# A fused attention and feed-forward kernel: the row of k's maxima is spread over the partitions by two DMAs through DRAM, not by four transposes, in batches 1 to 7

## The chip, the cores and the metric

The kernel runs on one core of one Trainium2 chip. The metric is the device time of one execution in microseconds (us); lower is better. The time before the change is the median of three runs.

## The reference

The reference is a linear attention (softmax of q over the head dimension, softmax of k over the sequence) followed by a two-layer feed-forward part. Cut to what matters:

```python
# q, k, v: (batch 8, heads 8, seq 576, head_dim 64), float32
q_s = softmax(q, axis=-1)                       # over the 64 of a head
k_s = np.exp(k - np.max(k, axis=2, keepdims=True))   # max over the sequence:
k_s = k_s / (np.sum(k_s, axis=2, keepdims=True) + 1e-9)  # one per batch, head, d
kv  = einsum('bhsd,bhse->bhde', k_s, v)
x   = einsum('bhsd,bhde->bhse', q_s, kv)        # to (4608, 512)
h   = x @ w_in                                  # 512 -> 2048
g   = h * erf(softplus(h))
out = g @ w_out                                 # 2048 -> 512
```

For each batch, the maximum of k over the sequence is 512 numbers: 8 heads of 64.

## The kernel before

**Work.** Tokens lie on the partitions when k and q are loaded: a batch has 576 tokens, 512 of them as 128 partitions x 4 and a tail of 64 that shares a tile with the other batch of its pair. Attention of a batch gives columns of x, already transposed; the feed-forward part takes them in blocks of 384 tokens, 12 blocks in all, each in 4 groups of the hidden dimension. That makes 48 items `n`. An item has a first product (`mm1`, lines 911 and, for the first four, 950), softplus and erf on ScalarE (both L343), a product on VectorE (L991) with two splittings into halves of 16 bits (L1005, L1009), and a second product (`mm2`, lines 1037 and 1028) that comes two items later. `mm1` multiplies blocks by Strassen's scheme of seven products; its PSUM banks are called pX, pY and pZ, with one buffer each. VectorE and ScalarE empty them into the tile H, and the next product of that bank waits for it: ScalarE's copies are L928, L930 and L938, VectorE's are L923, L925, L933 and L936.

**Order.** Batch 0 and the first four items are written out by hand in a list of steps. From there a loop over the items calls a generator, `attention`, which yields after each step of a batch; `pace` takes as many steps after each part of `mm2` as a table of shares sets. The tile framework then orders the instructions of each engine itself by a planner, so that a row can stand in another place than in the code; after that each engine runs its own list strictly in order. DMAs of activations, and the stores of the output, are all issued by SyncE (SP), one list as well.

**The steps of one batch around the change**, in `attention` (L639 on):

- `k_max` takes the maximum over the four tokens of each partition and the tail on VectorE (L496 to L500): a tile `kmax` of 128 x 512.
- `k_max_T` transposes `kmax` on TensorE in four pieces into a PSUM bank `kT` (L507); VectorE reduces that bank over the tokens (L511) to `km`, 128 x 4: column c, partition p holds the maximum of entry 128c + p.
- `k_max_rows` transposes each column of `km`, repeated 128 times, by four further transposes on TensorE into a PSUM bank `kB` (L520): every partition then holds the whole row of 512 maxima.
- VectorE subtracts `kB` from both halves of k, `k_0` and `k_1` (L654), and from the tail `kt` (L659). Between L511 and this stands whatever the planner put there.
- ScalarE takes the exponentials of `k_0`, `k_1`, `kt`, `q_0`, `q_1` and, for an odd batch, of the tail of q, `qt` (all L343).
- TensorE multiplies them with v into the banks `kv_0` and `kv_1` (L541; `kt` enters as `kv<-vtail,kt`).

The small PSUM tiles (`kT`, `kB`, `kv`, `qT`, `x` and so on) share two banks, tag `bk`. The tile `kmax`, its helper `k2` and the later `kvf` and `qTs` share two SBUF buffers, tag `qT`. Batch 0 takes the same functions by its own list of steps.

Of the kernel before, what the change touches and what calls it, by code (L numbers as in the profile page):

```python
# [9 lines left out]
F32 = mybir.dt.float32  # L10
# [46 lines left out]
def attn_moe_kernel(  # L57
# [9 lines left out]
    nc = tc.nc  # L67
    B, H, S, D = q.shape
    NTOK, DM = out.shape
    DFF = w_in.shape[1] // 2  # L70
    P = 128
# [4 lines left out]
    NC4 = DM // P  # L76
# [7 lines left out]
    GE = FG * T  # L84

    cp = ctx.enter_context(tc.tile_pool(name="cp", bufs=1))
    ch = ctx.enter_context(tc.tile_pool(name="ch", bufs=1))
    at = ctx.enter_context(tc.tile_pool(name="at", bufs=2))
    xp = ctx.enter_context(tc.tile_pool(name="xp", bufs=2))
# [248 lines left out]
    def act(out_, in_, func, chain=True, **kw):  # L338

        with ExitStack() as es:  # L340
            if chain and last[0] is not None:
                es.enter_context(tc.issue_after(last[0]))
            i = nc.scalar.activation(out_, in_, func, **kw)  # L343
        if chain:
            last[0] = i.ins
        return i
# [91 lines left out]
    def bank(name):  # L438
        return psa.tile([P, 512], F32, tag="bk", name=name)
# [4 lines left out]
    def hd(t):  # L444
        return t.rearrange("p h d -> p (h d)")

    def rows(t):
        return t.rearrange("p t h d -> p (t h) d")

    def q_sub(t, g, name):  # L450

        m = at.tile([P, g], F32, tag=f"qm{g}", bufs=1, name=f"{name}_m")
        nc.vector.tensor_reduce(m, t, axis=AX.X, op=ALU.max)
        nc.vector.tensor_tensor(
            t, t, m[:, :, None].to_broadcast([P, g, D]), op=ALU.subtract
        )
# [34 lines left out]
    def k_max(b, ks, kt):  # L491

        kmax = at.tile([P, H, D], F32, tag="qT", name=f"kmax_{b}")
        k2 = at.tile([P, 2, 4, D], F32, tag="qT", name=f"k2_{b}")
        for hf in range(2):
            nc.vector.tensor_tensor(k2, ks[hf][:, 0:2], ks[hf][:, 2:4], op=ALU.max)  # L496
            nc.vector.tensor_tensor(
                kmax[:, hf * 4:hf * 4 + 4, :], k2[:, 0], k2[:, 1], op=ALU.max
            )
        nc.vector.tensor_tensor(kmax[kt[1]], kmax[kt[1]], kt[0], op=ALU.max)  # L500
        return kmax

    def k_max_T(b, kmax):
        bk = bank(f"kT_{b}")
        km2 = hd(kmax)
        for c in range(NC4):
            nc.tensor.transpose(  # L507
                bk[:, c * P:(c + 1) * P], km2[:, c * P:(c + 1) * P], ident
            )
        km = at.tile([P, NC4], F32, tag="km", bufs=1, name=f"km_{b}")  # L510
        nc.vector.tensor_reduce(  # L511
            km, bk.rearrange("p (c s) -> p c s", c=NC4), axis=AX.X, op=ALU.max
        )
        return km

    def k_max_rows(b, km):

        bk = bank(f"kB_{b}")
        for c in range(NC4):
            nc.tensor.transpose(  # L520
                bk[:, c * P:(c + 1) * P], km[:, c:c + 1].to_broadcast([P, P]), ident
            )
        return bk.rearrange("p (h d) -> p h d", h=H)

    W = D + 1

    def kv_mm(b, hf):


        d, kt_ = bat[b], bat[b - b % 2]["kt"]  # L530
        bk = bank(f"kv_{b}_{hf}")
        for c in range(2):
            for t in range(TM + 1):
                for a in range(2):
                    h = 2 * c + a
                    if t < TM:
                        kk, vv = d["k"][hf][:, t, h, :], d["v"][hf][:, h, t, :]
                    else:

                        kk, vv = kt_[:, 4 * hf + h, :], vtail[:, 4 * hf + h, :]  # L540
                    nc.tensor.matmul(  # L541
                        bk[a * D:(a + 1) * D, c * W:(c + 1) * W], kk, vv,
                        start=(t == 0), stop=(t == TM),
                    )
        return bk
# [7 lines left out]
    def kv_norm(b, hf, bk):  # L553
        if b >= E32:
            if hf == 0:
                bat[b]["kvf"] = at.tile([P, NC4, D], F32, tag="qT", name=f"kvf_{b}")
            kvf = bat[b]["kvf"]
        bkv = bk[:, :2 * W].rearrange("p (c w) -> p c w", c=2)
        rd = at.tile([P, 2, 1], F32, tag="rd", bufs=1, name=f"rd_{b}_{hf}")
        nc.vector.tensor_scalar_add(rd, bkv[:, :, D:], 1e-9)  # L560
        nc.vector.reciprocal(rd, rd)
        cs = slice(2 * hf, 2 * hf + 2)
        if b >= E32:
            nc.vector.tensor_tensor(
                kvf[:, cs, :], bkv[:, :, :D], rd.to_broadcast([P, 2, D]), op=ALU.mult
            )
            return
        for a in range(2):
            ps = slice(a * D, (a + 1) * D)
            nc.vector.tensor_tensor(  # L570
                kv32[b][ps, cs, ps], bkv[ps, :, :D], rd[ps].to_broadcast([D, 2, D]),
                op=ALU.mult,
            )
# [68 lines left out]
    def attention(b):  # L642
        d, j, p = bat[b], b % 2, b // 2
        even = bat[b - j]
        tl = slice(j * TAIL, (j + 1) * TAIL)
        ks, qs, kt = d["k"], d["q"], even["kt"][tl]
        kmax = k_max(b, ks, (kt, tl))
        yield SHARES[0]
        km = k_max_T(b, kmax)
        q_sub(rows(qs[0]), 16, f"q_{b}_0")  # L650
        yield SHARES[1]
        kb = k_max_rows(b, km)
        for hf in range(2):
            nc.vector.tensor_tensor(  # L654
                ks[hf], ks[hf],
                kb[:, None, hf * 4:hf * 4 + 4, :].to_broadcast([P, TM, 4, D]),
                op=ALU.subtract,
            )
        nc.vector.tensor_tensor(kt, kt, kb[tl], op=ALU.subtract)  # L659
        yield SHARES[2]  # L660
        q_sub(rows(qs[1]), 16, f"q_{b}_1")
        if j == 1:
            q_sub(even["qt"], H, f"qt_{p}")
        yield SHARES[3]
        for t in (*ks, kt, qs[0], qs[1], *([even["qt"]] if j == 1 else [])):
            act(t, t, AF.Exp, chain=b > 1)
        yield SHARES[4]
        kv_norm(b, 0, kv_mm(b, 0))
        d["v"].append(load_half(v, "v", b, 1))
        q_norm(rows(qs[0]), 16, f"q_{b}_0", b)  # L670
        yield SHARES[5]
        kv_norm(b, 1, kv_mm(b, 1))
        if b + 1 < B:
            load_kv(b + 1)
        mx = kv_max(b)
        yield SHARES[6]
        kv_split(b, mx)
        yield SHARES[7]
        q_norm(rows(qs[1]), 16, f"q_{b}_1", b)
        if j == 1:  # L680
            q_norm(even["qt"], H, f"qt_{p}", b)
        yield SHARES[8]
        for i in ((3 * p + 1, 3 * p + 2) if j else (3 * p, 3 * p + 1)):
            while not x_free(i):
                yield 0
        if j == 1:
            qt2 = hd(even["qt"])
            bk = bank(f"qTt_{p}")
            for c in range(NC4):
                nc.tensor.transpose(  # L690
                    bk[:, c * P:(c + 1) * P], qt2[:, c * P:(c + 1) * P], ident
                )
            qT = q_evac(b, bk, f"qTt_{p}")
            if b + 1 < B:
                even_next = bat[b + 1]
                even_next["qt"] = load_tail(q, "qt", p + 1)
            yield SHARES[9]
            bk = bank(f"xt_{p}")
            x = xblock(p * NBK + 1)
            bk3 = bk.rearrange("p (c s) -> p c s", c=NC4)  # L700
            for a in range(2):
                for c in range(NC4):
                    cs = slice(c * P + a * TAIL, c * P + (a + 1) * TAIL)
                    x_mm(2 * p + a, c, bk[:, cs], qT[:, :, cs])
            for a in range(2 if b < E32 else 1):
                w = TAIL if b < E32 else P
                o = SM - T + a * TAIL
                x_put(
                    bk3[:, :, a * TAIL:a * TAIL + w], x[:, :, o:o + w],
                    bat[a]["sx"] if b < E32 else None,  # L710
                )
            yield SHARES[10]
        for c in range(NC4):
            hf, c2 = divmod(c, 2)
            qT = q_T(b, c, bank(f"qT_{b}_{c}"))
            if c2 == 1 and b + 1 < B:
                load_q(b + 1, hf)
            yield SHARES[11]
            bk = bank(f"x_{b}_{c}")
            x_mm(b, c, bk, qT)  # L720
            x_split(b, c, bk)
            if c == NC4 - 1:
                d["xdone"] = True
            yield SHARES[12]
# [464 lines left out]
```

## Time and profile before

| | |
|---|---|
| time, median of three runs | 862.84 us |
| the three runs | 860.36, 862.84, 862.9 us |
| span of the profiled execution, first to last instruction | 860.3 us |
| TensorE busy, share of the span | 825.6 us, 96% |
| VectorE busy | 637.1 us, 74% |
| ScalarE busy | 504.2 us, 59% |
| GpSimd busy | 17.6 us, 2% |
| mean DMA traffic | 65 GB/s |
| granted TensorE clock, mean over the span | 0.989 |

No time is recorded for the profiled execution by itself. Its span, from the first to the last instruction, is 0.1 us under the fastest of the three runs and 2.6 us under their median. In the rows of a timeline the first column is the start in us from the span's start and the second the time that the row lasts, with consecutive equal instructions merged; what stands in brackets at the end is the idle time of that engine ahead of the row and what ended it. Ends of matmuls are modelled and overlap the next instruction, so how long TensorE was really held by a group is read from the start of the group to the start of what follows. A group of matmuls in float32 counts two instructions for one in the code; the transposes count one.

### The profile page before, as it was taken

The numbers are of one execution on the slowest core, as the hardware profiler recorded it, in microseconds if no ns is written. First come the engines' busy times: TensorE is split into PE (matmuls) and PEld (weight loads), VectorE is DVE, ScalarE is ACT, GpSimd is POOL, SyncE is SP. The second block draws the span as 40 slices with busy tenths as digits, with TensorE's granted clock in tenths as the row PEclk, the third lists the DMA queues.
The fourth block names the chain that finished last, engine by engine and source line by source line (L and its number), as shares of the span: only waits on it lengthen the run. The fifth ranks groups of instructions, "written<-read, shape, count | busy, mean of one in ns | idle before, by whom it ended". The sixth has DMA issues, their size and how long they took to land.

```text
span 860.3 us, 15503 instructions
## 1 busy us (share of the span) xinstructions
PE 825.6 (96%) x6532; PEld 569.2 (66%) x6532; DVE 637.1 (74%) x921; ACT 504.2 (59%) x645; POOL 17.6 (2%) x37
## 2 busy tenths in 40 slices
PE   3999997999999999999999999999999999999997
PEld 2655556676766776776776677767776677777673
DVE  6899889998886779759866779858866656653543
ACT  2597677866554566565664466466655466453532
POOL 2010000000000000000000000000000000000000
PEclk8999999999999999999999999999999999999999
DMA  9996320032123302311140202311110000100100
GB/s 273 397 268 178 100 75 13 19 88 50 37 54 77 87 1 50 93 28 24 50 105 14 68 19 51 80 38 26 32 32 2 25 13 2 37 2 1 37 2 37
DMA packets 117381, 55.53 MB, mean 65 GB/s; under 512 B 106560, under 2 KB 108608, under 8 KB 117312
## 3 DMA queue, kind: packets, MB, share of 16 engines
q1 hardware_dynamic: 115136, 46.15, 20.6%
q0 software_dynamic: 2176, 8.39, 2.7%
q8 instruction: 51, 0.84, 0.4%
q14 instruction: 18, 0.15, 0.1%
HBM read 45.09 MB, written 9.44 MB: 63 GB/s over the span
## 4 chain that ended last, share of the span: by engine, by line
PE 67%; DVE 17%; ACT 10%; issue 2%; DMA 2%; SPq 1%; POOL 0%; ACTq 0%; DVEq 0%; POOLq 0%
PE o L1037 31%; PE pX L911 16%; PE pZ L911 8%; ACT G L343 4%; PE pY L911 4%; ACT L343 3%; PE kv L541 2%; DVE G L991 2%; PE x L631 2%; PE qT L616 2%; DVE H L1009 1%; DVE x L297 1%; PE o L1028 1%; DVE wi L297 1%; DVE H L1005 1%
## 5 line engine op out<-in xcount | busy, mean ns | idle before, releaser
L1037 PE MATMUL o<-wo,H 128*128 128x512 f16 x1512 | 348.0, 379 | 1.7 <-DVE H L1005 1.3
L911 PEld LDWEIGHTS <-wi 128*128 128x128 f16 x3696 | 309.5, 98 | 39.0 <-issue 17.4
L1037 PEld LDWEIGHTS <-H 128*128 128x128 f16 x1512 | 145.7, 98 | 150.1 <-DVE H L1005 1.8
L911 PE MATMUL pX<-x,wi 128*128 128x192 f16 x2112 | 204.8, 247 | 6.4 <-ACT H L930 3.0
L343 ACT ACT_TABLE_LOAD x104 | 133.4, 1283 | 8.5 <-DVE H L936 5.3
L991 DVE SCALAR_TENSOR_TENSOR G<-G,small,H 128x1536 f32<-128x1536 f32 x44 | 80.0, 1818 | 65.8 <-ACT G L343 65.5
L911 PE MATMUL pZ<-x,wi 128*128 128x192 f16 x1056 | 102.9, 246 | 0.9 <-DVE H L936 0.5
L938 ACT COPY H<-pX 128x384 f32<-128x384 f32 x44 | 20.9, 476 | 138.0 <-PE pX L911 133.0
L343 ACT ACTIVATE G<-H,U 128x768 f32<-128x768 f32 (+1 forms) x60 | 72.9, 1231 | 24.4 <-DVE H L936 23.8
L1009 DVE TENSOR_TENSOR H<-G,H 128x1536 f16<-128x1536 f32 x42 | 73.8, 1757 | 1.1
L343 ACT ACTIVATE G<-G 128x1536 f32<-128x1536 f32 x48 | 71.2, 1484 | 0.5
L1028 PE MATMUL o<-wo,G 128*128 128x512 f32 x144 | 66.7, 604 | 0.0
L911 PE MATMUL pY<-x,wi 128*128 128x192 f16 x528 | 51.8, 248 | 1.6 <-DVE H L923 1.6
L442 ACT ACTIVATE x<-x 128x384 f32<-128x384 f32 (+1 forms) x52 | 17.6, 386 | 54.4 <-PE x L631 51.9
L923 DVE COPY H<-pY 128x384 f32<-128x384 f32 x44 | 24.4, 554 | 31.4 <-PE pY L911 31.3
L1028 PEld LDWEIGHTS o<-wo,G 128*128 128x128 f32 x144 | 26.3, 193 | 26.5 <-issue 25.8
L297 DVE SCALAR_TENSOR_TENSOR x<-x,x 128x768 f16<-128x768 f32 (+1 forms) x44 | 37.1, 850 | 5.8 <-ACT x L296 5.7
L1005 DVE CAST H<-G 128x1536 f16<-128x1536 f32 x42 | 40.1, 955 | 0.7
L296 ACT ACTIVATE x<-x 128x768 f16<-128x768 f32 (+1 forms) x44 | 32.9, 761 | 11.4 <-DVE x L387 11.4
L1053 DVE TENSOR_SCALAR ob<-o,V 128x512 f32<-128x512 f32 x29 | 21.7, 748 | 23.1 <-PE o L1037 23.1
L936 DVE TENSOR_TENSOR H<-pZ,H 128x384 f32<-128x384 f32 x44 | 24.3, 552 | 19.3 <-PE pZ L911 19.3
L925 DVE TENSOR_TENSOR H<-pX,H 128x384 f32<-128x384 f32 x44 | 24.4, 555 | 15.3 <-PE pX L911 14.9
(182 smaller groups left out, 804.2 us busy)
## 6 DMA issues: line engine op xcount, KB each, us to landing
out_dram<-ob SPq DMA_DIRECT2D x32, 256.0 KB, 2.3
vbuf<-in_v_dram SPq DMA_DIRECT2D x60, 128.0 KB, 3.1
q<-in_q_dram SPq DMA_DIRECT2D x56, 128.0 KB, 3.2
k<-in_k_dram SPq DMA_DIRECT2D x56, 128.0 KB, 3.3
wo<-in_moe_w_in_dram SPq DMA_DIRECT2D x4, 1024.0 KB, 16.9
wi<-in_moe_w_out_dram POOLq DMA_DIRECT2D x2, 1024.0 KB, 8.3
wi<-in_moe_w_in_dram SPq DMA_DIRECT2D x2, 1024.0 KB, 8.0
raw<-in_moe_w_out_dram POOLq DMA_DIRECT2D x2, 1024.0 KB, 7.9
```

What stands on the lines that cost most here:

```text
L296: nc.scalar.activation(hi, src, AF.Copy, scale=s)
L297: nc.vector.scalar_tensor_tensor(lo, src, s, hi, op0=ALU.mult, op1=ALU.subtract)
L343: i = nc.scalar.activation(out_, in_, func, **kw)
L911: nc.tensor.matmul(o, w[wl][:, c, a * P:(a + 1) * P], x[:, xl, xi, c, :], start=(new and a == 0 and c == 0 and i == 0), stop=(c == 1 and i ...
L923: nc.vector.tensor_copy(C[0, 0], bank2("Y"))
L925: add(C[0, 0], bank2("X"), C[0, 0], op=ALU.add)
L936: add(C[0, 1], bank2("Z"), C[0, 1], op=ALU.add)
L991: nc.vector.scalar_tensor_tensor(flat(s["G"]), flat(s["G"]), (GB if n in OUT32 else GA)[:, g:g + 1], flat(s["H"]), op0=ALU.mult, op1=ALU.mult,
L1005: nc.vector.tensor_copy(flat(s["gh"]), flat(s["G"]))
L1009: nc.vector.tensor_tensor(flat(s["gl"]), flat(s["G"]), flat(s["gh"]), op=ALU.subtract)
L1028: nc.tensor.matmul(o, s["G"][:, a, ts_], w[:, a, :], start=(first_ and a == 0), stop=(last_ and a == FG - 1),)
L1037: nc.tensor.matmul(o, s[gt][:, a, ts_], w[wl][:, a, :], start=(first_ and a == 0 and i == 0), stop=(last_ and a == FG - 1 and i == 2),)
```

## The change

A DRAM pool with two buffers is added. For batches 1 to 7, `k_max_rows` and its four transposes are replaced by `k_max_spread`, which is called right after `k_max_T`: SyncE stores `km` to a row of 512 numbers in DRAM, and then loads this row into all 128 partitions of a new SBUF tile `kB`. Batch 0 keeps the four transposes.

```diff
+    dr = ctx.enter_context(tc.tile_pool(name="dr", bufs=2, space=bass.MemoryType.DRAM))
...
+    def k_max_spread(b, km):
+
+        row = dr.tile([1, DM], F32, tag="km", name=f"kmd_{b}")
+        nc.sync.dma_start(row.rearrange("o (c p) -> (o p) c", c=NC4), km)
+        kb = at.tile([P, DM], F32, tag="qT", name=f"kB_{b}")
+        nc.sync.dma_start(kb, row.to_broadcast([P, DM]))
+        return kb.rearrange("p (h d) -> p h d", h=H)
...
         kmax = k_max(b, ks, (kt, tl))
         yield SHARES[0]
         km = k_max_T(b, kmax)
+        kb = k_max_spread(b, km)
         q_sub(rows(qs[0]), 16, f"q_{b}_0")
         yield SHARES[1]
-        kb = k_max_rows(b, km)
         for hf in range(2):
```

The subtraction therefore reads `kB` from SBUF and not from PSUM, and waits for a DMA and not for TensorE. `kB` takes one more turn in the two buffers `qT`, and the turn of `kB` in the two PSUM banks `bk` is gone. On SP the two DMAs stand ahead of the loads of v's second half, and in batches 5 and 7 ahead of four stores of the output. Lines after the new function have moved by nine or ten.

The planner also moves other rows. In batches 2, 3, 4 and 6 the order on VectorE between the reduction L511 and the subtractions is the same as before. At three places other rows change.

ScalarE in batch 5, from the erf of an item (`G<-G`) to the exponentials of that batch and the copies of the banks pZ and pX into H. Before:

```order
L343 ACTIVATE G_3916<-G_3916 128x1536
L928 COPY H_3920<-pZ_3985 128x2x192
L343 ACT_TABLE_LOAD
L343 ACTIVATE k_0_3185<-k_0_3185 128x1024
L930 COPY H_3920<-pX_3935 128x2x192
L343 ACTIVATE k_1_3190<-k_1_3190 128x1024
L343 ACTIVATE kt_2213<-kt_2213 64x512
L343 ACTIVATE q_0_3478<-q_0_3478 128x1024
L343 ACTIVATE q_1_3659<-q_1_3659 128x1024
L343 ACTIVATE qt_2358<-qt_2358 128x512
L938 COPY H_3920<-pX_3935 128x2x192
```

And now (L344 is the L343 of before, L937, L939 and L947 are L928, L930 and L938):

```order
L344 ACTIVATE G_3918<-G_3918 128x1536
L344 ACT_TABLE_LOAD
L344 ACTIVATE k_0_3183<-k_0_3183 128x1024
L344 ACTIVATE k_1_3188<-k_1_3188 128x1024
L344 ACTIVATE kt_2212<-kt_2212 64x512
L344 ACTIVATE q_0_3476<-q_0_3476 128x1024
L344 ACTIVATE q_1_3657<-q_1_3657 128x1024
L344 ACTIVATE qt_2357<-qt_2357 128x512
L937 COPY H_3922<-pZ_3982 128x2x192
L939 COPY H_3922<-pX_3937 128x2x192
L947 COPY H_3922<-pX_3937 128x2x192
```

The copies of pZ and of the first pX have moved from among the exponentials to behind all six of them; batch 7 has the same move.

TensorE at the same place, from the last `mm2` product of an item (bank `o_2`) to `kv_0`. Before, the pX product that waits for the copy L930 stood between `o_1` and `o_2`, further up:

```order
L1037 MATMUL o_2_3551<-wo_95,H_3603 128x512
L541 MATMUL kv_0_4062<-vbuf,k_0_3185 64x65 x8
L541 MATMUL kv_0_4062<-vtail,kt_2213 64x65 x2
L541 MATMUL kv_0_4062<-vbuf,k_0_3185 64x65 x8
L541 MATMUL kv_0_4062<-vtail,kt_2213 64x65 x2
L911 LDWEIGHTS wi_90
L911 MATMUL pZ_3985<-x_5_3444,wi_90 128x192
```

Now it stands inside `kv_0`:

```order
L1046 MATMUL o_2_3549<-wo_97,H_3601 128x512
L550 MATMUL kv_0_4059<-vbuf,k_0_3183 64x65 x8
L550 MATMUL kv_0_4059<-vtail,kt_2212 64x65 x2
L550 MATMUL kv_0_4059<-vbuf,k_0_3183 64x65
L920 LDWEIGHTS wi_92
L920 MATMUL pX_3937<-x_5_3442,wi_92 128x192
```

The 12 matmuls of that pX product have moved behind `o_2` and the first eleven of the twenty `kv_0` matmuls; batch 7 has the same move.

VectorE in batch 1, from the reduction to `km` to the subtractions, among the unpacking of weights (`sg<-wo`, L209 to L215) and the normalising of q (`q_0_r`). Before:

```order
L511 TENSOR_REDUCE km_438<-kT_433 128x4
L460 TENSOR_REDUCE q_0_r<-q_0_189 128x16
L654 TENSOR_TENSOR k_0_318<-k_0_318,kB_443 128x1024
L654 TENSOR_TENSOR k_1_323<-k_1_323,kB_443 128x1024
L659 TENSOR_TENSOR kt_105<-kt_105,kB_443 64x512
```

And now:

```order
L512 TENSOR_REDUCE km_440<-kT_435 128x4
L461 TENSOR_REDUCE q_0_r<-q_0_191 128x16
L210 TENSOR_SCALAR sg_615<-wo_97 128x1024
L463 TENSOR_SCALAR q_0_r<-q_0_r 128x16
L210 TENSOR_SCALAR sg_615<-wo_98 128x1024
L466 RECIPROCAL q_0_r<-q_0_r 128x16
L213 SCALAR_TENSOR_TENSOR sg_615<-wo_97,sg_615 128x1024
L467 TENSOR_TENSOR q_0_191<-q_0_191,q_0_r 128x1024
L216 SCALAR_TENSOR_TENSOR sg_615<-wo_97,sg_615 128x1024
L663 TENSOR_TENSOR k_0_320<-k_0_320,kB_444 128x1024
L663 TENSOR_TENSOR k_1_325<-k_1_325,kB_444 128x1024
L668 TENSOR_TENSOR kt_107<-kt_107,kB_444 64x512
```

Seven rows of unpacking and normalising have moved in front of the subtractions; on TensorE the `kv` products of batch 1 have moved behind the first eight `mm2` products of item 1.

## The prediction

> **What bounds the kernel now.** I read the page's busy shares and chain first, then single stretches, then the instructions around the transposes in each batch, and last the landing times of the DMAs.
>
> ```profile
> PE 825.6 (96%) x6532; PEld 569.2 (66%) x6532; DVE 637.1 (74%) x921; ACT 504.2 (59%) x645; POOL 17.6 (2%) x37
> PE 67%; DVE 17%; ACT 10%; issue 2%; DMA 2%; SPq 1%; POOL 0%; ACTq 0%; DVEq 0%; POOLq 0%
> ```
>
> TensorE (PE) is busy nearly all the time, but only two thirds of the chain that ended last is its own. So it depends on the stretch, seen in two windows (length, then busy time of PE, PEld, DVE, ACT, POOL):
>
> ```profile
> 65.00:100.00 35.00, 34.90 (x180) 19.03 (x178) 34.64 (x54) 22.00 (x44) 2.46 (x4) 1.00 0.59 161
> 250.00:640.00 390.00, 387.28 (x3416) 277.58 (x3414) 297.74 (x439) 224.21 (x275) 2.53 (x8) 1.00 0.20 49
> ```
>
> In the first, which holds batch 1, TensorE and VectorE are both full. In the second, which holds batches 4 to 7, TensorE idles 2.7 us of 390: time taken from it there is earned, and every wait of it is paid.
>
> **What is removed: 28 transposes.**
>
> ```profile
> L520 PE MATMUL kB<-ident,km x32: 272/273/475, 10.6 to 612.1; 128*128 128x128 f32 x32
> ```
>
> Of these 32, four belong to batch 0 and stay. One takes 273 ns, but they overlap. Four hold TensorE for 0.44 us, from their start to that of the next product (416.03 to 416.47 in batch 5, rows below). All seven batches together could give 7 x 0.44 = 3.1 us. The Trainium skill ("TensorE: Matmul & The Clock Gate", Part 4: PE-mode transpose) gives about 275 ns for a transpose inside a kernel; the trace agrees on one alone, and by that figure the 28 would be an estimated 7.7 us. I take 0.44 us, since starts of neighbours show what TensorE can do with the time.
>
> **What is added: two DMAs in a row.** Call L the time from the end of the reduction L511 to the landing of `kB`. The trace has neither transfer; the nearest rows are these: the output's store of 128 rows of 2 KB, the shape of the new load turned round; the loads of k in runs of 64 numbers, 512 runs each as the new store has 512 single numbers; and such loads in the window 46:56, beside weights of 1 MB.
>
> ```profile
> DMA to landing us min/median/max: 2.0/2.3/4.1
> out_dram<-ob SPq DMA_DIRECT2D x32, 256.0 KB, 2.3
> k<-in_k_dram SPq DMA_DIRECT2D x56, 128.0 KB, 3.3
> k<-in_k_dram SPq DMA_DIRECT2D x8, 128.0 KB, 7.0
> 416.23 0.75 DVE L1053 TENSOR_SCALAR ob<-o,V 128x512 f32<-128x512 f32 x1 [2.03 <-PE o L1037]
> 417.01 9.95 SPq L1056 DMA_DIRECT2D out_dram<-ob  x4
> ```
>
> The first line is that of the stores (L1056). SP issues 0.03 us after what it waited for ends (416.98, 417.01). So L is 3.3 + 2.3 + 2 x 0.03 = 5.7 us, my value: each transfer by the row nearest in number of runs. The ends are twice the stores' minimum and maximum, 4.1 and 8.3 us. The Trainium skill ("DMA: Bandwidth & Descriptors", Latency and other measured facts) puts the fixed cost of a DMA at about 2 us, which would make L an estimated 4 us, near my lower end.
>
> **Batch 1.**
>
> ```profile
> 68.90 0.68 DVE L511 TENSOR_REDUCE km<-kT 128x4 f32<-128x512 f32 x1
> 69.50 1.21 DVE L460 TENSOR_REDUCE q_r<-q 128x16 f32<-128x1024 f32 x1
> 69.64 0.41 PEld L520 LDWEIGHTS kB<-ident,km 128*128 128x128 f32 x4 [0.53 <-DVE km L511]
> 70.13 0.81 PE L950 MATMUL pZ<-x,wi 128*128 128x384 f32 x2
> 73.72 0.18 DVE L462 TENSOR_SCALAR q_r<-q_r 128x16 f32<-128x16 f32 x1
> 78.80 0.58 DVE L570 TENSOR_TENSOR kvbd<-kv,rd 64x128 f32<-64x128 f32 x2
> ```
>
> Here TensorE waits 0.53 us for `km` and then transposes for 0.49 (69.64 to 70.13): up to 1.0 us earned. The subtractions now stand behind L460 and seven more rows, which before ran from 73.72 to 78.80 with two short ones among them: some 1.1 + 4.9 = 6 us of cover for L. Beside the weights, one transfer at 7.0 us and one at 2.3 make L 9.4 us, and VectorE, full in this stretch, would idle 3.4. Ends -1.0 and +3.4; I take -0.5, half of what TensorE could earn, as VectorE is just as full.
>
> **Batches 2 and 3.**
>
> ```profile
> 139.52 0.68 DVE L511 TENSOR_REDUCE km<-kT 128x4 f32<-128x512 f32 x1
> 148.51 2.08 PE L911 MATMUL pX<-x,wi 128*128 128x192 f16 x12 [3.05 <-ACT H L930]
> 153.89 1.21 DVE L654 TENSOR_TENSOR k<-k,kB 128x1024 f32<-128x1024 f32 x1
> 232.21 0.68 DVE L511 TENSOR_REDUCE km<-kT 128x4 f32<-128x512 f32 x1
> 239.40 2.35 DVE L654 TENSOR_TENSOR k<-k,kB 128x1024 f32<-128x1024 f32 x2
> 241.76 0.69 PE L541 MATMUL kv<-vbuf,k 128*64 128x65 f32 x16 [1.03 <-ACT k L343]
> ```
>
> In both TensorE soon waits for something else (3.05 us for ScalarE's copy, 1.03 for the exponential of k), so the 0.44 us turns into a longer wait: nothing earned. Nothing is lost either: VectorE comes to the subtraction 13.7 us after `km` in batch 2 and 6.5 us in batch 3 (232.89 to 239.40), later than 5.7. Above 6.5 batch 3 pays in full. Term: 0, or L - 6.5.
>
> **Batches 4 and 6.** Batch 6 has the same order of rows as batch 4; I count it as the same.
>
> ```profile
> 319.41 0.69 DVE L511 TENSOR_REDUCE km<-kT 128x4 f32<-128x512 f32 x1 [2.47 <-PE kT L507]
> 325.12 2.35 DVE L654 TENSOR_TENSOR k<-k,kB 128x1024 f32<-128x1024 f32 x2
> 326.37 2.19 ACT L343 ACTIVATE k<-k 128x1024 f32<-128x1024 f32 x2 [3.20 <-DVE k L654]
> 327.97 0.69 PE L541 MATMUL kv<-vbuf,k 128*64 128x65 f32 x16
> ```
>
> TensorE is full, so 0.44 us is earned. VectorE is at the subtraction 5.0 us after `km` (320.10 to 325.12), so L of 5.7 moves it back by 0.7. ScalarE waits for it, and TensorE for ScalarE: the first exponential ends at about 326.37 + 2.19/2 = 327.46, now 328.16. TensorE comes to `kv` 0.44 earlier, less the five pZ matmuls that the planner has put in front (5/12 of 0.99 us, by the 12 pX of 421.04 to 422.03 below): at 327.94. So `kv` waits from L = 5.0 + 0.5 = 5.5 on, for 0.2 us at 5.7. Term: -0.44 + (L - 5.5), each; at 5.7 both together -0.5.
>
> **Batches 5 and 7.** Batch 7 has the rows of batch 5; counted as the same.
>
> ```profile
> 410.34 0.68 DVE L511 TENSOR_REDUCE km<-kT 128x4 f32<-128x512 f32 x1
> 416.03 0.60 PE L520 MATMUL kB<-ident,km 128*128 128x128 f32 x4
> 416.34 1.49 ACT L343 ACTIVATE G<-G 128x1536 f32<-128x1536 f32 x1
> 416.47 1.15 PE L911 MATMUL pZ<-x,wi 128*128 128x192 f16 x12
> 418.21 1.28 ACT L343 ACT_TABLE_LOAD   x1
> 419.45:425.90 6.45, 5.30 (x7) 1.00 0.01 3
> 420.46 0.46 ACT L930 COPY H<-pX 128x384 f32<-128x384 f32 x1
> 421.04 1.15 PE L911 MATMUL pX<-x,wi 128*128 128x192 f16 x12
> 421.87 0.69 DVE L659 TENSOR_TENSOR kt<-kt,kB 64x512 f32<-64x512 f32 x1
> 422.03 2.75 PE L1037 MATMUL o<-wo,H 128*128 128x512 f16 x12
> 424.71 0.69 PE L541 MATMUL kv<-vbuf,k 128*64 128x65 f32 x16
> 426.03 1.16 PE L911 MATMUL pZ<-x,wi 128*128 128x192 f16 x12
> ```
>
> The windowed line is ScalarE's L343 alone: the six exponentials, 5.3 us. Before, the copy L930 slips in after the first of them and TensorE runs on without a wait. Now both copies come last: erf ends at 417.83, table load to 419.1, exponentials to 424.4, two copies of 0.46 to 425.3. TensorE is earlier by 0.44, and `o_2` by the 0.99 of the pX product that has gone behind it: `o_2` at 420.60, 2.68 us long (422.03 to 424.71), `kv` from 423.28. Of the 1.32 us of `kv` (424.71 to 426.03), 11/20 pass, 0.73, and at 424.0 pX stands before a bank that is free at 425.3: 1.3 us of wait. With pX 0.99 and the rest of `kv` 0.59 the next pZ starts at 426.9, not at 426.03: 0.9 us lost, the saved transposes already counted. Through L this grows only when the exponential of `kt`, whose turn is at 421.2, is held up: `kt` is subtracted 2.35 + 0.75 + 0.69 = 3.8 us after landing, so from L = 421.2 - 3.8 - 411.0 = 6.4 on. Term: +0.9 + (L - 6.4), each; at 5.7 both +1.8.
>
> What else moves costs nothing as far as the rows go: SP issues the two DMAs in gaps, and the four stores behind them in batch 5 went out at 417.01, when both new DMAs have been issued (`km` plus 0.03 and 3.3). The subtraction reads SBUF in place of PSUM.
>
> **Sum.** -0.5 + 0 + 0 - 0.5 + 1.8 = +0.8 us. The profiled span is 860.3 us; the median shown, 862.84, lies 2.5 above. On the median I forecast 863.6 us. A measurement of this kernel can tell about 0.3%, 2.6 us, from no change; this is within.
>
> **Rivals.**
>
> *Slower: the landing of `kB` becomes the wait.* One mechanism, in batches 3 to 7: VectorE stands at L654 for the second DMA, ScalarE for VectorE, TensorE at `kv`. It decides from about L = 6.5, where the sum is -0.5 + 2 x 0.56 + 2 x 1.0 = +2.6; each further us adds five. At 7.0 us it is -0.5 + 0.5 + 2 x 1.06 + 2 x 1.5 = +5.1 (868 us); at 8.3, -0.5 + 1.8 + 2 x 2.36 + 2 x 2.8 = +11.6 (874). For it: the maximum of 4.1 and the 7.0 beside weights, and that single numbers of 4 bytes are further from any row than the rest. Against it: median 2.3 and few bytes in these stretches (DMA share 0.20). The Trainium skill ("DMA: Bandwidth & Descriptors", Rules for kernel authors) warns that a strided last dimension becomes one descriptor per element and that small transfers are mostly overhead; the store is such a one, no run here shows its price, and by the rule it leans this way.
>
> *Faster: each transpose is worth its 273 ns.* If TensorE's rate and not its gaps were bound by them, batches 1 and 4 to 7 would earn 5 x 4 x 0.273 = 5.5 us: 857 us, less the 2.6 of waits in batches 5 and 7, 860. That is also where the time ends if the copies don't hold TensorE up: -1.0 - 4 x 0.44 = -2.8. Against both: the starts 0.44 apart, and copies that stand behind all six exponentials.
>
> That the change does not do what it says is excluded by the new order: 28 transposes are gone.
>
> **How the numbers follow.** L below 6.5 and the waits as worked out: 0.52, the forecast. Slower: 0.36, as batches 4 and 6 are past their edge at 5.7 and batches 3, 5 and 7 within 0.8 us of theirs. Faster: 0.12. The range leaves out most of the faster case and the tail above L = 7.4: 860 to 870 us. The forecast's own range, from L = 4.1 with batch 1 at -1.0 (-0.1) to L = 6.5 (+2.6), is 862.7 to 865.5.
>
> **What would show it.** No `kB` rows on TensorE outside batch 0. Landing of the two new DMAs near 3.3 and 2.3 us. VectorE idle at L654 of about 0.7 us on a DMA in batches 4 and 6, none in 3. TensorE waiting 1.3 us for ScalarE's copy of pX in batches 5 and 7. The prediction is wrong if L is above 6.5, or if TensorE does not wait there.

## The result: 57 us slower

The changed kernel takes 919.23 us (median of 5 runs, 916.55 to 919.63) against 860.52 us (5 runs, 858.92 to 862.9): a ratio of 1.066, 95% interval 1.064 to 1.068. The prediction was 863.6 us, range 860 to 870. The profiled execution took 919.44 us, its span is 917.3 us, against 860.3 us before: 57.0 us more. The two medians lie 58.7 us apart; the rows below are those of the two profiled executions.

The profile after: busy shares and the chain that ended last, by engine and by line.

```profile
PE 835.3 (91%) x6504; PEld 574.7 (63%) x6504; DVE 637.5 (69%) x921; ACT 505.8 (55%) x646; POOL 17.2 (2%) x37
PE 61%; DVE 14%; DMA 11%; ACT 8%; issue 2%; SPq 2%; POOL 0%; ACTq 0%; DVEq 0%
PE o L1046 24%; PE pX L920 15%; PE pZ L920 7%; DMA kmd<-km 6%; PE o L1037 4%; ACT G L344 3%; PE pY L920 3%; PE kv L550 3%; DMA kB<-kmd 3%; ACT L344 3%; DVE G L1000 2%; DVE H L1018 2%; SPq L409 2%; PE x L640 1%; PE qT L625 1%
```

DMA has gone from 2% of the chain to 11%, and the two new transfers stand in it by name: the store `kmd<-km` 6%, the load `kB<-kmd` 3%. TensorE's idle time (span less busy) has grown from 34.7 to 82.0 us, by 47.3; its busy time has grown too, by 9.7 us, with 28 instructions fewer. Together that is the 57.0.

The waits name the path. The columns are engine, tile and line that waited, what for, us in total and how often:

```profile
ACT k L344 <- DVE k L663: 54.5, 6, 11.8
DVE k L663 <- DMA kB<-kmd: 52.8, 6, 10.5
PEld kv L550 <- ACT k L344: 32.0, 5, 8.3
```

VectorE stands at the subtraction for `kB` and ScalarE for VectorE, six times each. TensorE stands at `kv` for ScalarE in five of the six (PEld is its loading of weights). In batch 3 it comes to a product of the bank pX first, and waits for VectorE's addition L942, which stands behind the subtraction on VectorE's list:

```profile
260.88 0.48 PE L920 MATMUL pX<-x,wi 128*128 128x192 f16 x2 [9.01 <-DVE H L942]
```

None of the waits for `kB` was there before. Why it takes so long, from the lines of the store (L529) and the load (L531), in this order:

```profile
DMA to landing us min/median/max: 8.2/8.7/11.8
DMA to landing us min/median/max: 3.3/4.5/4.8
```

The store's median is 8.7 us where the prediction had 3.3, the load's 4.5 where it had 2.3. One batch in order of time, batch 4, the counterpart of the rows at 319.41 to 327.97 of before:

```profile
337.89 0.69 DVE L512 TENSOR_REDUCE km<-kT 128x4 f32<-128x512 f32 x1 [2.47 <-PE kT L508]
338.61 0.38 SPq L529 DMA_DIRECT2D kmd<-km  x1
348.47 0.33 SPq L531 DMA_DIRECT2D kB<-kmd  x1
352.15 2.36 DVE L663 TENSOR_TENSOR k<-k,kB 128x1024 f32<-128x1024 f32 x2 [8.47 <-DMA kB<-kmd]
354.52 1.20 PE L550 MATMUL kv<-vbuf,k 128*64 128x65 f32 x16 [8.03 <-ACT k L344]
```

From the end of the reduction (338.58) to the subtraction are 13.6 us; this is L. TensorE waits 8.03 us, and then takes 1.20 us for a group of 16 matmuls that took 0.69 before. The windows of this stretch say why (length; busy time of PE, PEld, DVE, ACT, POOL; granted clock; DMA share; GB/s):

```profile
347.30:348.40 1.10, 0.00 (x0) 0.00 (x0) 0.00 (x0) 0.00 (x0) 0.00 (x0) 1.00 0.00 0
348.40:352.20 3.80, 0.00 (x0) 0.00 (x0) 0.04 (x1) 0.00 (x0) 0.00 (x0) 0.90 0.18 71
352.20:356.00 3.80, 1.48 (x19) 1.34 (x20) 3.38 (x4) 2.51 (x3) 0.00 (x0) 0.50 0.00 0
```

After the idle stretch TensorE is granted half its clock. In windows of 1 us the clock is 1.00 up to 351, 0.71 from 351 to 352, and 0.50 from there to 358: it falls some 4.9 us into the wait, and is full again some 3.7 us after TensorE has started to work. The Trainium skill ("TensorE: Matmul & The Clock Gate", Part 1: The HAM clock gate) describes this, half rate after at least one idle window of about 3.4 us. The trace agrees on the half, and 4.9 us is more than one such window.

A last view, of DMA alone from the store's issue to its landing, 338.5 to 348.4 in 40 slices of 0.25 us:

```profile
DMA  0000630000000000000000000000000000000000
DMA packets 528, 0.00 MB, mean 0 GB/s; under 512 B 528, under 2 KB 528, under 8 KB 528
kmd<-km SPq DMA_DIRECT2D x1, 2.0 KB, 9.8
```

The 512 packets (and 16 more) are done within two slices, 0.9 to 1.4 us after the issue. The other 8 us pass with the DMA engines idle in the records, before the landing is reported; in batches 2, 3, 5, 6 and 7 the same view shows the same. So it is not the time that the packets take on the engines. What takes the time behind them is in no record.

### The profile page after: what moved, and what is told of

Its sections match the earlier page's. It is cut to its first block, busy times and chain, and to the rows that moved or that the text cites. A ratio compares the mean times of both kernels' runs of the same rounds, so it can differ in the third digit from the quotient of the medians.

```text
span 917.3 us, 15466 instructions
## 1 busy us (share of the span) xinstructions
PE 835.3 (91%) x6504; PEld 574.7 (63%) x6504; DVE 637.5 (69%) x921; ACT 505.8 (55%) x646; POOL 17.2 (2%) x37
## 4 chain that ended last, share of the span: by engine, by line
PE 61%; DVE 14%; DMA 11%; ACT 8%; issue 2%; SPq 2%; POOL 0%; ACTq 0%; DVEq 0%
PE o L1046 24%; PE pX L920 15%; PE pZ L920 7%; DMA kmd<-km 6%; PE o L1037 4%; ACT G L344 3%; PE pY L920 3%; PE kv L550 3%; DMA kB<-kmd 3%; ACT L344 3%; DVE G L1000 2%; DVE H L1018 2%; SPq L409 2%; PE x L640 1%; PE qT L625 1%
## 5 line engine op out<-in xcount | busy, mean ns | idle before, releaser
L920 PE MATMUL pX<-x,wi 128*128 128x192 f16 x2112 | 208.3, 249 | 19.7 <-DVE H L942 10.3
L947 ACT COPY H<-pX 128x384 f32<-128x384 f32 x44 | 20.9, 476 | 149.1 <-PE pX L920 133.4
L344 ACT ACTIVATE G<-H,U 128x768 f32<-128x768 f32 (+1 forms) x60 | 72.8, 1231 | 24.5 <-DVE H L945 23.9
L344 ACT ACTIVATE G<-G 128x1536 f32<-128x1536 f32 x48 | 71.3, 1484 | 0.5
L550 PE MATMUL kv<-vbuf,k 128*64 128x65 f32 x480 | 27.1, 265 | 34.3 <-ACT k L344 29.7
L663 DVE TENSOR_TENSOR k<-k,kB 128x1024 f32<-128x1024 f32 x14 | 16.6, 1222 | 52.8 <-DMA kB<-kmd 52.8
L550 PEld LDWEIGHTS kv<-vbuf,k 128*64 128x64 f32 x480 | 23.1, 175 | 42.2 <-ACT k L344 32.0
L344 ACT ACTIVATE k<-k 128x1024 f32<-128x1024 f32 x14 | 14.8, 1056 | 55.0 <-DVE k L663 54.5
```

What stands on the lines that cost most here:

```text
L550: nc.tensor.matmul(bk[a * D:(a + 1) * D, c * W:(c + 1) * W], kk, vv, start=(t == 0), stop=(t == TM),)
L920: nc.tensor.matmul(o, w[wl][:, c, a * P:(a + 1) * P], x[:, xl, xi, c, :], start=(new and a == 0 and c == 0 and i == 0), stop=(c == 1 and i ...
L947: nc.scalar.copy(C[1, 0], bank2("X"))
```

## Experiments

Two theories stood at the start. *A: the landing of the store, and by it the wait for `kB`, is the loss.* *B: the two extra DMAs cost by being there, on SP's list or among other transfers, or the planner's other order costs.*

### Shapes of the store and of the load, nobody waiting

The kernel before, with one unread store per batch and one unread load of 256 KB, other shapes in each batch. Some of the stores: 512 numbers 2 KB apart (batch 1), as in the change (batch 2), and 128 runs of 16 B (batch 5):

```diff
+        if b == 1:
+            dst, src = t(DM, 512).rearrange("(c p) w -> p c w", c=NC4)[:, :, 0:1], km[:, :, None]
+        elif b == 2:
+            dst, src = t(1, DM).rearrange("o (c p) -> (o p) c", c=NC4), km
...
+        elif b == 5:
+            dst, src = t(1, DM).rearrange("o (p c) -> (o p) c", c=NC4), km
...
```

> The kernel before, with its four transposes, and in each batch 1 to 7 one store from SBUF to DRAM that nobody reads, at the place of the change's store: batches 1 and 4: 512 single numbers of 4 bytes, 2 KB apart; batch 2: the change's own store, 512 single numbers side by side in 2 KB; batch 3: 512 single numbers 64 bytes apart; batch 5: 128 runs of 16 bytes side by side in 2 KB; batch 6: 128 single numbers side by side; batch 7: 128 runs of 64 bytes. At the end of each batch one load of 256 KB that nobody reads: 128 different rows of 2 KB in odd batches, the same row 128 times in even ones. Theory A (single numbers that fall on the same few memory lines are written one after the other, so the landing goes by how many writes fall there): batch 2 lands in 8 to 9 us, batches 3 and 4 in under 5, batch 5 in about 4, batch 6 in about 4, batch 7 in under 3. Rival B (every write of 4 bytes is slow, wherever it falls): batches 2, 3 and 4 all land in 8 to 9 us, 5 and 6 in about 4. Rival C (any small store to DRAM with this many partitions takes this long): all between 7 and 10. For the loads: if the same row is what makes the load slow, 4 us or more in even batches and under 3 in odd ones; if not, alike.

A look at other spacings followed, stores only:

> The kernel before with one unread store each in batches 2 to 7, to tell what makes the 512 single numbers slow. Batch 2: 512 single numbers 8 bytes apart (8 to a line of 64 bytes); batch 3: 16 bytes apart (4 to a line); batch 6: 32 bytes apart (2 to a line); batch 4: 512 single numbers 8 bytes apart, with the four of one partition next to each other; batch 5: 256 single numbers side by side (16 to a line); batch 7: 128 runs of 8 bytes side by side (8 to a line). Theory A (writes into the same line of 64 bytes go one after the other): batch 5 lands in 7 to 9 us, batches 2, 4 and 7 in about 4 to 5, batch 3 in about 3, batch 6 in 2. Rival (it is only the side by side that is slow, or a threshold): 2, 3, 4, 6 and 7 all under 3, batch 5 over 7.

The rows of the stores, each from the window of its issue (last number: us to landing). First run, batches 2, 3, 5 and 6: 512 numbers side by side, 512 numbers 64 B apart, 128 runs of 16 B, 128 numbers side by side.

```profile
sd<-km SPq DMA_DIRECT2D x1, 2.0 KB, 8.6
sd<-km SPq DMA_DIRECT2D x1, 2.0 KB, 1.9
sd<-km SPq DMA_DIRECT2D x1, 2.0 KB, 1.4
sd<-km SPq DMA_DIRECT2D x1, 0.5 KB, 7.1
```

Second run, batches 2, 3 and 6: 512 numbers 8, 16 and 32 B apart.

```profile
sd<-km SPq DMA_DIRECT2D x1, 2.0 KB, 3.5
sd<-km SPq DMA_DIRECT2D x1, 2.0 KB, 2.9
sd<-km SPq DMA_DIRECT2D x1, 2.0 KB, 2.1
```

512 numbers from the same kind of tile land in 1.9 or in 8.6 us, by where they go. Their count matters little, against the theory, which had 4 us for 128 numbers: 128 side by side take 7.1 us, 256 take 8.0, 512 take 8.6; and 512 apart by 2 KB take 2.0 (5.4 beside the weights in batch 1). In 64 bytes fall 16 writes, 8, 4, 2 or 1 at spacings of 4, 8, 16, 32 and 64 B, and the landing falls with them, 8.6, 3.5, 2.9, 2.1, 1.9. Order within the row is not it: 512 numbers 8 B apart, with the four of a partition next to each other, take 3.2, and 128 runs of 8 B side by side take 3.2 as well. One shape does not fit: 128 runs of 64 B, from another tile, take 3.1 us, more than the 1.4 of the runs of 16 B. Each of these is a single store.

That writes into the same 64 bytes are taken one after another is my reading and not shown: no shifted start was tried, and the largest step, 8.6 to 3.5 us, lies between numbers that touch and numbers with a gap, so the touching itself may be the cause. What is shown is that the place of the numbers in DRAM decides, far more than their count.

The unread loads: same row for all partitions 4.9, 3.6, 3.8 us (batches 2, 4, 6), 128 different rows 3.7, 3.8, 3.7, 2.6 (batches 1, 3, 5, 7). Reading one row 128 times is not what makes the load slow; the shape costs 2.6 to 4.9 us either way. The two kernels took 864.77 and 861.58 us in one run each, against medians of 863.5 and 862.16 us for the kernel before: such DMAs, when no engine and no other DMA waits for them, cost little.

### The two DMAs of the change, unread

The transposes are back, and the subtraction reads their `kB`; the store and the load run too, into a tile that nobody reads. The order on TensorE, VectorE and ScalarE is that of before.

```diff
         km = k_max_T(b, kmax)
-        kb = k_max_spread(b, km)
+        k_max_spread(b, km)
...
+        kb = k_max_rows(b, km)
```

> The kernel before with its four transposes, plus the two DMAs of the change, store and load, into a tile that nobody reads; the order on TensorE, VectorE and ScalarE is that of before in every row. Theory (the loss is the wait for the second DMA and what follows from it): the store still lands in 8 to 9 us and the load in about 4, and the time is that of before within 0.5%. Rival (the DMAs themselves, by holding up SP's list or the loads and stores behind them, cost the time): 890 us or more.

872.03 us (4 runs) against 863.5 (7 runs), ratio 1.009, interval 1.007 to 1.012. The store still takes 8.5 to 13.8 us. So the DMAs, with nobody waiting for `kB`, cost some 8 us. This is not a share to be taken off the 57: in the changed kernel the wait for `kB` falls into the same stretch. The rows of batch 1, SP's list and TensorE:

```profile
70.68 0.38 SPq L529 DMA_DIRECT2D kmd<-km  x1
84.47 0.34 SPq L531 DMA_DIRECT2D kB<-kmd  x1
84.92 2.57 SPq L409 DMA_DIRECT2D vbuf<-in_v_dram  x4
88.96 1.45 PE L550 MATMUL kv<-vbuf,k 128*64 128x65 f32 x15 [9.94 <-DMA vbuf<-in_v_dram]
```

SP waits 13.8 us with the load at the head of its list, and the loads of v behind it go out at 84.92; before they went out at 74.16. TensorE then waits 9.94 us for v. In the later batches nothing is lost: the reduction starts 13.7 us later than before in batch 2, 14.0 in batch 3, 12.7 in batch 7. B holds, in batch 1 alone.

### Runs of 16 bytes

The store writes the four numbers of a partition side by side: 128 writes of 16 B. First the view of `kB` was turned round for it:

```diff
-        nc.sync.dma_start(row.rearrange("o (c p) -> (o p) c", c=NC4), km)
+        nc.sync.dma_start(row.rearrange("o (p c) -> (o p) c", c=NC4), km)
...
+        return kb.rearrange("p (a d c) -> p c a d", a=2, c=NC4)
...
```

> The changed kernel with one difference: the row lies in DRAM in the order in which the partitions hold it, so that the store has 128 runs of 16 bytes in place of 512 single numbers; VectorE reads the loaded row through a view with a stride, in two instructions for each half. Theory (the landing of kB sets the loss, and of it the number of small writes): the store lands in about 4 us in place of 8.7, L falls from 13 to about 8.5, and each of the six batches that waited gives back some 4.5 us: about 919 - 6 x 4.5 = 892 us, between 885 and 900. Rival (a DRAM round trip takes its 13 us whatever its shape): within 1% of the changed kernel, 919.

887.13 us (4 runs), ratio 1.028, interval 1.025 to 1.030. Against 57 us the loss is now 24, but a second thing had changed: the subtraction reads `kB` with a stride of 16 B, and is slower for it. Groups of the subtraction here, and of after:

```profile
L664 DVE TENSOR_TENSOR k<-k,kB 128x512 f32<-128x512 f32 x28 | 29.3, 1096 | 7.6 <-DMA kB<-kmd 7.6
L663 DVE TENSOR_TENSOR k<-k,kB 128x1024 f32<-128x1024 f32 x14 | 16.6, 1222 | 52.8 <-DMA kB<-kmd 52.8
```

Half as many numbers per instruction take nearly as long, 12.7 us more in all. The wait for `kB` went from 52.8 to 7.6 us, though. The time is within the expected 885 to 900 us, but not for the expected reason: the store landed in 2.1 us (median) and not in 4, and the slower subtraction took back what that gained. So the turn was moved to where it is free, into the input of the first transposes:

```diff
+        km4 = km2.rearrange("q (p c) -> q c p", c=NC4)
...
-                bk[:, c * P:(c + 1) * P], km2[:, c * P:(c + 1) * P], ident
+                bk[:, c * P:(c + 1) * P], km4[:, c, :] if b and SPREAD else km2[:, c * P:(c + 1) * P], ident
```

> The changed kernel, its order on TensorE, VectorE and ScalarE the same in every row, with the store as 128 runs of 16 bytes: the first transposes take every fourth column of the maxima, so that km already holds the row in the order of DRAM, and VectorE reads kB as in the changed kernel. Theory (the loss is L, and the terms of the prediction hold with the right L): the store lands in about 2.1 us and the load in about 4, L is 6.2 us, and by the prediction's terms (-0.5 in batch 1, -0.44 + 0.7 in 4 and 6, +0.9 in 5 and 7) the time is about 2 us above that of before: 863 to 868 us. Rival (the new order costs by itself more than was reckoned, most of all ScalarE's copies behind the exponentials in batches 5 and 7): 870 us or more although the landing is short.

866.3 us against 862.16 (12 runs), ratio 1.005, interval 1.003 to 1.007, with the rows of TensorE, VectorE and ScalarE in the order of after. So of the 57 us some 53 belong to how the store's numbers lie in DRAM. The profile of the same kernel comes from further runs.

> The changed kernel with the store in 128 runs of 16 bytes once more, for a readable profile. First theory (the chain from the reduction to the landing of kB sets the time, and the rest of the prediction's working holds): store 1.4 to 2, load 4.0 to 4.5, so about 6 us in all; VectorE waits for kB less than 1 us in batches 4 and 6, none in 3, and TensorE waits about 1.3 us for ScalarE's copies in batches 5 and 7; time 863 to 867. Rival (part of the loss is the load itself or the order, whatever the store does): VectorE still waits 2 us and more for kB in several batches.

865.78 us (8 runs) against 861.27 (19), ratio 1.005, interval 1.003 to 1.007. Landing of the store and of the load, the waits for `kB` (all, then batches 4 and 7), and waits of TensorE in batches 5 and 7 (L942 is the copy L930 of before, L945 the addition L933):

```profile
DMA to landing us min/median/max: 1.4/2.1/2.7
DMA to landing us min/median/max: 3.2/3.9/4.9
L666 DVE TENSOR_TENSOR k<-k,kB 128x1024 f32<-128x1024 f32 x14 | 16.6, 1220 | 7.2 <-DMA kB<-kmd 7.2
325.72 2.36 DVE L666 TENSOR_TENSOR k<-k,kB 128x1024 f32<-128x1024 f32 x2 [0.30 <-DMA kB<-kmd]
613.96 2.36 DVE L666 TENSOR_TENSOR k<-k,kB 128x1024 f32<-128x1024 f32 x2 [2.79 <-DMA kB<-kmd]
424.99 1.15 PE L923 MATMUL pX<-x,wi 128*128 128x192 f16 x12 [0.94 <-ACT H L942]
428.54 1.15 PE L923 MATMUL pX<-x,wi 128*128 128x192 f16 x12 [0.57 <-DVE H L945]
622.11 1.15 PE L923 MATMUL pX<-x,wi 128*128 128x192 f16 x12 [0.94 <-ACT H L942]
```

L is about 6 us now (5.4 in batch 4: 320.34 to 325.72), the size that the prediction had; VectorE waits 0.30 us in batch 4 and 0.42 in batch 6, none in 3. The rest of its 7.2 us are 1.20 in batch 1, 2.47 in batch 5 and 2.79 in batch 7, so the sign of the rival, waits of 2 us and more, is there in two batches. ScalarE does not wait for VectorE there, since its table load ends later. But VectorE then works without a gap up to the addition L945, and TensorE waits for that: 0.57 us in batch 5, 0.90 in batch 7. TensorE waits for the copy at the pX products of batches 5 and 7, as the prediction said, 0.94 us each.

### The load in two halves

```diff
-        nc.sync.dma_start(kb, row.to_broadcast([P, DM]))
+        for i in range(2):
+            r = slice(i * 256, i * 256 + 256)
+            nc.sync.dma_start(kb[:, r], row[:, r].to_broadcast([P, 256]))
```

> As c2b, with the load cut into two loads of 256 maxima each, so that the first subtraction can begin when the first half is there. First theory: a landing is mostly a fixed time, so the first half lands 0.3 to 1 us sooner and the second at the same time or later; the time is within 3 us of c2b either way (862 to 868). Rival (the landing goes by the bytes): the first half lands after half the time, 2 us, and c6 is as fast as the kernel before.

867.11 us (6 runs), ratio 1.006, interval 1.004 to 1.009: no gain. The fourteen loads of 128 KB have a median of 3.9 us, the seven of 256 KB of the run above 3.9 too: between these two sizes the landing does not go by the bytes.

### Batches 5 and 7 apart from the others

The last two runs divide the 4.5 us that were left, with the runs of 16 bytes in some batches and the transposes in the others (`if b in SPREAD`).

> The 16-byte runs in batches 1, 2, 3, 4 and 6 only; batches 5 and 7 keep the transposes, and with them ScalarE's copies stand in their old places between the exponentials. First theory (of the 4.5 us that c2b lies over the kernel before, the two waits for ScalarE's and VectorE's copies in batches 5 and 7 are 1.6 and 2.0): at most 1.5 us over the kernel before. Rival (the loss is the DMAs themselves, a like share for each batch): five sevenths of 4.5, that is 3.2 us over.

> The other way round: the 16-byte runs in batches 5 and 7 only, with ScalarE's copies behind all six exponentials there; the other batches as before. First theory: 3 to 4.5 us over the kernel before, and TensorE waits about 0.9 us for ScalarE's copy of pX in each of the two. Rival (a like share for each batch): two sevenths of 4.5, 1.3 us over.

Without 5 and 7: 863.11 us (12 runs) against 861.96 (23), ratio 1.001, interval 0.999 to 1.003. With 5 and 7 only: 864.22 (12 runs), ratio 1.003, interval 1.002 to 1.004, that is +1.5 to +3.7 us. Five batches cost nothing that can be measured; the two with the moved copies cost 2.3 us, less than the 3 to 4.5 expected, more than a like share of 1.3. As the 4.5 are themselves known to 2.8 to 5.9 only, a like share could be up to 1.7 and is not excluded. Nor are the copies alone in this: VectorE waits 2.50 and 2.12 us for `kB` in these two batches. TensorE's waits for the copy there, batches 5 and 7 of the second kernel (L943 is the copy L930 of before):

```profile
424.23 1.15 PE L924 MATMUL pX<-x,wi 128*128 128x192 f16 x12 [0.94 <-ACT H L943]
622.39 1.15 PE L924 MATMUL pX<-x,wi 128*128 128x192 f16 x12 [0.94 <-ACT H L943]
```

In the first kernel TensorE has no such wait in either stretch.

### Without any spreading

Batches 1 to 7 subtract each partition's own maximum: the 28 transposes are gone, with no DMA in their place.

```diff
-        kb = k_max_rows(b, km)
+        kb = kmax
```

> Leaves part of the work out: batches 1 to 7 subtract each partition's own maximum instead of the spread one, so the four transposes per batch are gone, and no DMA and no wait take their place. It is the most that any way of spreading could win here. First theory (the transposes were worth 0.4 to 0.5 us in three batches and nothing in the others): 0 to 2 us under the kernel before. Rival (each of the 28 transposes was worth its 273 ns): 7.6 us under it.

861.62 us (12 runs) against 861.27, ratio 0.9995, interval 0.998 to 1.001: between 1.6 us won and 0.8 lost; 7.6 are excluded. This is not the worth of the transposes by itself. With no DMA in it, the planner has put ScalarE's two copies behind all six exponentials here too, and TensorE waits for the second of them, in batches 5 and 7:

```profile
420.11 1.15 PE L911 MATMUL pX<-x,wi 128*128 128x192 f16 x12 [1.21 <-ACT H L930]
617.72 1.15 PE L911 MATMUL pX<-x,wi 128*128 128x192 f16 x12 [1.20 <-ACT H L930]
```

So the move comes from taking the transposes away and not from the DMAs, and up to 2.4 us that the transposes gave back may be lost again in these waits. Its subtractions also stand elsewhere on VectorE's list, as they need not wait for `km`. A kernel without transposes and with the old order was not run. In the planner's order there was nothing measurable for a DMA to win, and no version here beats the kernel before.

### A batch ahead: a miss

To give L a whole batch to pass, the maxima, the store and the load of the next batch were moved into the batch before (`k_ahead(b + 1)` behind an item), first with the transposes as a control and then with the DMAs; a buffer of the output's was given up for the room.

> The kernel before, with its four transposes, but in batches 2 to 7 the maximum of k and its first transposes are done a batch ahead, after the second of the four x products of the batch before; the output tiles have two buffers in place of three to make room. It is the control for the next kernel. Expected by every theory: within 1% of before, as VectorE and TensorE do the same work.

> The control with the two DMAs of the change, single numbers and all, in batches 2 to 7, issued a batch ahead; batch 1 keeps its transposes. Theory (only the exposed landing costs): the store still takes 8 to 9 us, VectorE does not wait for kB, and the time is that of the control less at most 6 x 0.44 = 2.6 us. Rival (the slow store costs also where nothing waits for it, by holding up SP's list): 5 us or more above the control.

873.71 us (ratio 1.013, interval 1.010 to 1.016) for the control, 922.31 us (1.071, 1.068 to 1.073) with the DMAs. The control is already outside the 1% that every theory gave it. With the DMAs the planner drew the subtraction up behind the reduction again, and the wait is as before:

```profile
DVE k L675 <- DMA kBs<-kmd: 51.3, 6, 11.7
```

So this did not separate the landing from the wait, and says nothing on whether a cover of a batch would hide it.

## Why the prediction was wrong

**The step that failed is L, and in it the store.** "Each transfer by the row nearest in number of runs" took 3.3 us from the loads of k, with 512 runs as the store has 512 numbers. The number of runs does not set the landing: 128 numbers side by side take 7.1 us, 512 apart 1.9. What counts is where they fall in DRAM, side by side or apart, and for 4-byte numbers side by side no row of before has a likeness. The load's 2.3 us, from the output's stores, was 4.5; a load of 256 KB took longer here than a store of as many bytes. L was 13 to 15 us, not 5.7, and past both ends of the estimate (4.1 and 8.3), which were twice the minimum and maximum of one store's shape and so no bounds for another shape. The rival "the landing of `kB` becomes the wait" was the right mechanism, with 0.36 for all its sizes; its price was worked out to L = 8.3 only, and left batch 1 at -0.5 at every L, though by the prediction's own cover of 6 us that batch pays from there on.

The Trainium skill ("DMA: Bandwidth & Descriptors", Rules for kernel authors), weighed in that rival, says that a strided last dimension becomes a descriptor per element. The 528 packets agree, and the rule pointed the right way; but the store with its numbers 64 B apart has 528 packets too and lands in 1.9 us, so the number of descriptors is not the price. The fixed cost of a DMA of about 2 us in the Trainium skill ("DMA: Bandwidth & Descriptors", Latency and other measured facts) agrees with the spread stores (1.9, 2.0) and the 16-byte runs (1.4 to 2.7), not with the store as made.

**The terms as functions of L held at this size of L.** With L from the rows of after (end of the reduction to the start of the subtraction), by batch, the prediction's term (for batch 1, L less its cover of 6 us, as in its upper end) and the cost as the growth of the distance from one batch's reduction to the next:

| batch | L | VectorE idle for `kB` | the prediction's term at this L | cost measured |
|---|---|---|---|---|
| 1 | 15.2 | 9.26 | 9.2 | 9.1 |
| 2 | under 13.7 | 0 | 0 | -0.5 |
| 3 | 13.3 | 6.66 | 6.8 | 7.5 |
| 4 | 13.6 | 8.47 | 7.6 | 9.3 |
| 5 | 13.7 | 10.52 | 8.2 | 10.9 |
| 6 | 13.1 | 7.96 | 7.1 | 8.7 |
| 7 | 13.1 | 9.94 | 7.6 | 9.6 |
| sum | | 52.8 | 46.5 | 54.6 |

The remaining 2.4 us of the 57.0 lie ahead of the first reduction (71.33 against 68.90), where no instruction of the change has run yet. The cover of 13.7 us in batch 2 and of 6.5 in batch 3 came out as read from the rows of before. The 8.1 us between the two sums were in no term. TensorE's busy time from batch 1's reduction on is 781.9 us against 771.6, 10.4 more, with the clock halved after each wait. In batch 4 the clock is half for some 3.7 us of work; half of that for each of the six waits is an estimated 11 us. That is about the difference, though it was not tested by a run of its own.

**The transposes: not contradicted.** 0.44 us in each of batches 4 to 7 and 0.5 in batch 1 were counted as earned, 2.3 us. Without any DMA the prediction's terms, the moved copies with them, add up to -0.5 - 2 x 0.44 + 2 x 0.9 = +0.4 us. The kernel without spreading lies between -1.6 and +0.8, so it agrees with this sum, but does not measure the 0.44 by itself. The rival that had each transpose worth its 273 ns came to 5.5 us won less 2.6 of these waits, 2.9, and that is outside.

**ScalarE's copies: the right mechanism, and a second path that was missed.** The wait of TensorE in batches 5 and 7 was forecast at 1.3 us, with 0.9 lost in each. The kernel without spreading has this wait with 1.21 and 1.20 us and no DMA. With L of the forecast's size (the 16-byte runs) the wait for the copy is 0.94 us, and a second one of 0.57 and 0.90 for VectorE's addition follows, behind VectorE's own wait for `kB`. The prediction let L count in these batches only by the exponential of `kt`, from 6.4 us on; at an L of 5.6 and 6.0 it already counts by VectorE's list. The two batches cost 2.3 us against the 1.8 forecast; how much of it is the copies and how much this second path was not separated. In after, with its longer L, the wait for the copy is 2.57 and 2.58 us.

**SP: "costs nothing" was wrong in batch 1.** The gap was read with L of 5.7 us; there the store takes 11.8, and everything behind the load on SP's list waits with it. In the unread pair, where the store took 13.8 us, that cost some 8 us by itself; in after it hides behind the wait for `kB`.

Had L been right the forecast would have been about 909 us (862.8 + 46.5), in place of 863.6. Conversely, with the store in 16-byte runs the prediction's 0.8 us meets a measured 4.5 (2.8 to 5.9): of this, 2.3 are found in batches 5 and 7 and 1.1, no more than the measurement's doubt, in the others; the rest was not settled.

## What to carry to other kernels

The small store here was priced by how its pieces lay at the destination, not by its bytes, its number of pieces or its packets' time: write neighbouring bytes from one partition together, or leave 64 B between single numbers (the load of such a row was not tried), and put any turn of the data into an operation that takes a stride for free. Before a transfer replaces a few matmuls, ask what the matmuls cost now (here nothing measurable) and how long the engine at the other end can wait; a round trip through DRAM took 5 to 7 us here at best, and ended on the path of three engines. Taking instructions out can also make the planner move others: here the moved copies took back what the transposes may have given. Where a duration's nearest row differs in kind, the range belongs to the unknown shape and not to the spread of the known one.

## What the runs showed of the hardware

- 512 numbers of 4 bytes into one row of 2 KB land after 8.2 to 13.8 us, although in batches 2 to 7 their packets were through about 1.4 us after the issue; 64 B apart they landed in 1.9 us (one store), as 16-byte runs in 1.4 to 2.7. The Trainium skill ("DMA: Bandwidth & Descriptors", Specifications) says that transfers below 512 B are read-modify-write; all these shapes are below it, so this alone does not tell 8.6 from 1.9.
- A load of 256 KB into 128 partitions takes 2.6 to 5.5 us to land, whether from one row (3.1 to 5.5) or from 128 (2.6 to 3.8); of 128 KB from one row as long, 3.9 by the median.
- Some 4.9 us into a wait of 8 us TensorE's granted clock fell from 1.00 to 0.50; it stayed there for the next 3.7 us of work, and 16 matmuls took 1.20 us instead of 0.69.
- A subtraction whose second operand has a stride of 16 B took 1.10 us for 512 numbers per partition, against 1.22 for 1024 without.
